# H3 and squared-ReLU layers in fp32 on one core: operands, residuals and rows of a joint unit of 1024 tokens are moved in time and place

## The chip, the cores and the metric

The kernel runs on one core of one Trainium2 chip. The metric is the device time of one execution in microseconds (us); lower is better. PE is TensorE, DVE VectorE, ACT ScalarE, POOL GpSimd, and SP the queue engine that issues the transfers.

## The reference

Two equal layers over 2048 tokens of width 1024. Each is an H3 block and a squared-ReLU MLP, with residuals:

```python
def H3(q, k, v):            # q = layernorm(x); A_k, A_v, A_shift_k, A_ssm_k, A_ssm_D are inputs
    kv = causal_conv4(k, shift_k) * v
    y = long_causal_conv(kv, ssm_k) + kv * ssm_D        # per channel, over 2048 tokens
    return q * y
def MLP(x):                 # w1 is 1024 x 3584, w2 is 3584 x 1024
    r = relu(x @ w1 + b1)
    return (r * r) @ w2 + b2
for _ in range(2):
    x = x + H3(layernorm(x), ...)
    x = x + MLP(layernorm(x))
```

All is fp32. The change touches the MLP only.

## The kernel before

**Matmuls.** An fp32 operand is held as two fp32r tiles: hi, a rounded copy that ACT writes, and lo, the raw value minus hi, a subtraction on DVE or POOL. A product is three matmuls, hi·hi, hi·lo and lo·hi (`mm3`, L344 to L346); each of the three moves 512 columns. The program is a list of steps, one for each weight tile of 128x512, and a step is 12 matmuls.

**Units.** The MLP runs in units of (layer, 512 tokens), in an order written out by hand. Units 5 and 6, the last block of layer 0 and the third of layer 1, are one joint unit of 1024 tokens, multiplied in the manner of Strassen and Winograd with seven products instead of eight. It has three parts:

- *Part 1* (`ja`, a = 1 and 2, 28 steps): for each of 14 pairs p of hidden blocks, x11·w11 and then x12·w21 in the same bank. After the first, ACT copies the bank (`j_p1`, L1906) and the copy goes to memory (PD, L1907); after the second, ACT rectifies the sum (L1901, L1902) and `j_c11` stores it as a result (RD, L1912). Meanwhile the other block's rows are loaded (`j_rows_load`), normalised on ACT (`j_rows_norm`, L1853) and turned (L1873), and DVE makes sums of blocks for part 2.
- *Part 2* (`ja`, a = 6, 5, 7, 4, 3, 70 steps): five more products for each p, with weights that are sums of four blocks of w1. The blocks are loaded at L1057, two into the ring `wr` and two into `jr`, with one more row of the ring for the fifth sum; DVE makes the sums (L1045 to L1048). ACT copies product 6's bank (`j_keep`, L1924) before product 7 goes on in it. Seven combined results go to memory as operands of part 3.
- *Part 3* (`jb`): seven products, in the order 0, 4, 5, 2, 1, 6, 3, of 14 steps each. `r_advance` loads their operands (L1970), ACT casts hi (L1981), and DVE or POOL subtracts (L1989), into a ring of 4 tiles for product 0 and of 7 later; from product 1's middle on (n ≥ 70) every second subtraction is POOL's. After each product `j_evict` (L2037, DVE) adds its banks into one of four residual groups: product 0 into (0,0), 4 into (1,1), 5 and 2 into (0,1), 1 into (0,0) again, 6 into (1,1), 3 into (1,0). The residuals come by `j_acc_load` (L2016) into `acc`, `yh`, `yl`, `fy` and `fg`, b2 by `load_b2` (L1825) into `px`; POOL adds b2 (`j_b2`, L2024). Products 0, 5, 6 and 3 use one side of four banks, 4, 2 and 1 the other, so a side's next product waits for the eviction of its last one. After product 1, `j_next` puts the next unit's norms and combination (L705 to L723, L819, L820) on DVE.

**What sets the order.** `lag.at(n, f)` runs f n steps later; within a step the program issues due work, weights, then operands. Weights are loaded eight steps ahead, cast four ahead (L1101) and subtracted three ahead (L1109). A weight used more than once is kept in memory as a split pair after its first use (WD): such a pair is loaded whole, 512 KB (L1097), unless it is in the set `single`; a raw tile is 256 KB. Raw tiles, blocks for sums and the results of `j_c11` share the ring `wr` of eight rows (`row()`). All these transfers go through SP's one queue in program order, and each engine works through its own list in order.

Of the kernel before, what the change touches and what calls it, by code (L numbers as in the profile page):

```python
# [11 lines left out]
F32 = mybir.dt.float32  # L12
F32R = mybir.dt.float32r
# [6 lines left out]
S, D, F = 2048, 1024, 3584  # L20
P = 128
T = 512
NT = T // P
NB = S // T
KT = D // P
FT = F // P
FC = 7
# [8 lines left out]
ORDER = [(0, 0), (1, 0), (0, 1), (0, 2), (1, 1), (0, 3), (1, 2), (1, 3)]  # L36
# [17 lines left out]
JU = 5  # L54
WMAKE = 4
NP = FT // 2
# [4 lines left out]
R_LOAD, R_HI, R_LO = 8, 4, 3  # L61
# [187 lines left out]
def tile_h3_mlp(ctx: ExitStack, tc: tile.TileContext, q, kT, vT, shk, ssmT, ssmD, w1, b1, w2, b2,  # L249
                fwd_t, pro_t, inv_t, sgn_t, out):  # L250
    nc = tc.nc
    V, A, G, PE, SY = nc.vector, nc.scalar, nc.gpsimd, nc.tensor, nc.sync
# [4 lines left out]
    cv = ctx.enter_context(tc.tile_pool(name="cv", bufs=1))  # L257
# [9 lines left out]
    X1 = [dram.tile([P, NT, D], F32, name=f"x1{b}") for b in range(NB)]  # L267
# [12 lines left out]
    def mkfg(shape, dt=F32):  # L280
        return cv.tile(shape, dt, name="fg", bufs=3)
# [246 lines left out]
    def prod_stream():  # L528
# [381 lines left out]
    steps, wsrc, single = [], [], set()  # L910

    def add(kind, u, c, a, i, tts=ALL, w=None):
        if w is None:
            w = len(wsrc)
            wsrc.append((kind, c, a, i))
        steps.append((kind, u, c, a, i, tts, w))
# [17 lines left out]
    def add_joint(u):  # L934
        for n in range(0, NP, 2):
            for kh in range(2):
                for p in (n, n + 1):
                    wsrc.append(("m1", 2 * p // FC, 2 * p % FC, kh))
                    add("ja", u, 0, kh + 1, p, w=len(wsrc) - 1)
        seq = [(6, 0), (5, 0), (7, 0)]  # L940
        for p in range(NP):
            more = p + 1 < NP
            seq += [(6, p + 1)] * more + [(4, p), (3, p)] + [(5, p + 1), (7, p + 1)] * more
        for j, p in seq:
            wsrc.append(("s", 0, j, p))
            add("ja", u, 0, j, p, w=len(wsrc) - 1)
        for j in JORD:
            for p in range(NP):
                f = 2 * p + (j > 0)
                wsrc.append(("m2", f // FC, int(j == 2), f % FC) if j < 3 else ("t", p, (j - 4) % 4, 0))  # L950
                add("jb", u, 0, j, p, w=len(wsrc) - 1)
# [194 lines left out]
    mw = ctx.enter_context(tc.tile_pool(name="mw", bufs=1))  # L1146
# [689 lines left out]
    rowp, xop, jst, jrows, jacc, rt, rptr = [], {}, {}, [], {}, {}, {"load": 0, "hi": 0, "lo": 0}  # L1836

    def jrow():
        if not rowp:
            n = jst["n"] = jst.get("n", -1) + 1  # L1840
            t = pre.tile([P, D], F32, name="px", bufs=2) if n % 3 == 2 else ml.tile([P, D], F32, name="acc", bufs=NT)
            rowp.extend((t[:, 0:512], t[:, 512:]))
        return rowp.pop(0)

    def j_rows_load(b):
        for tt in range(NT):
            jrows.append(ml.tile([P, D], F32, name="acc", bufs=NT))
            SY.dma_start(jrows[tt], X1[b][:, tt])

    def j_rows_norm(rn, tt):  # L1850
        for h in range(2):
# [55 lines left out]
        SY.dma_start(PD[p], t)  # L1907

    def j_c11(o, p):
        x = row()  # L1910
        rectify(x["t"], o, 2 * p)
        SY.dma_start(RD[0][p], x["t"])  # L1912
        drop(x)
# [42 lines left out]

    rseq = [(j, p) for j in JORD for p in range(NP)]

    def r_ring(n):
        return 4 if n < NP else 7  # L1960

    def r_load():
        n = rptr["load"]
        rptr["load"] += 1
        if n == 0:
            jst["xr"] = mw.tile([P, 8, T], F32, name="xh", bufs=1)
            jst["xs"] = mw.tile([P, 4, 2, T], F32R, name="xl", bufs=1)
        t = jst["xr"][:, n % 8] if n < NP else ml.tile([P, T], F32, name="rh", bufs=FC + 1)
        j, p = rseq[n]
        SY.dma_start(t, RD[j][p])  # L1970
        rt[n] = [t]

    def r_hi():
        n = rptr["hi"]
        rptr["hi"] += 1
        if n < NP:
            t = jst["xs"][:, n % 4]
        else:
            nm, m = (("cx", 2), ("cg", 2), ("cp", 3), ("cx", 2), ("cp", 3), ("cg", 2), ("cp", 3))[n % 7]
            t = cv.tile([P, 2, T], F32R, name=nm, bufs=m)  # L1980
        A.copy(t[:, 0], rt[n][0])  # L1981
        rt[n].append(t)

    def r_lo():
        n = rptr["lo"]
        rptr["lo"] += 1
        raw, t = rt[n]
        E = G if n >= 5 * NP and n % 2 else V
        E.tensor_sub(t[:, 1], raw, t[:, 0].bitcast(F32))  # L1989

    def r_advance(m):
        N = len(rseq)
        while rptr["lo"] < rptr["hi"] and rptr["lo"] <= m + R_LO:
            r_lo()
        while rptr["hi"] < min(rptr["load"], N) and rptr["hi"] <= m + R_HI and rptr["hi"] - r_ring(rptr["hi"]) < m:
            r_hi()
        while rptr["load"] < N and rptr["load"] <= m + R_LOAD and rptr["load"] - 8 < rptr["lo"]:
            r_load()
        while m >= 0 and rptr["lo"] <= m:
            if rptr["load"] <= rptr["hi"]:  # L2000
                r_load()
            if rptr["hi"] <= rptr["lo"]:
                r_hi()
            r_lo()
        rt.pop(m - 1, None)

    def j_acc_load(k):
        if k == 0:
            ts = [ml.tile([P, D], F32, name="acc", bufs=NT) for _ in range(NT)]
        else:  # L2010
            ts = [cv.tile([P, D], F32, name=nm, bufs=1) for nm in ("yh", "yl", "fy")]
        for tt in range(NT):
            for h in range(2):
                d = slice(h * 512, (h + 1) * 512)
                a = jacc[k, tt, h] = ts[tt][:, d] if tt < len(ts) else mkfg([P, T])
                SY.dma_start(a, X1[ORDER[JU + k][1]][:, tt, d])  # L2016
        if k == 0:
            jst["acc"] = ts

    def j_b2(st, k):  # L2020
        for tt in range(NT):
            for h in range(2):
                a = jacc[k, tt, h]
                G.tensor_add(a, a, st["t"][:, h * 512:(h + 1) * 512])  # L2024

    def j_banks(j):
        if j in JOPEN or j in (5, 6, 3, 2):
# [90 lines left out]
    for sb in range(1, NB):  # L2118
        if WIN[sb] > lo_u:
# [3 lines left out]
            n = sum(last_step[u] + 1 - start_step[u] - 19 * (1 - PREP_PACE) for u in range(lo_u, hi_u))  # L2123
# [16 lines left out]
    for s, (k, u, c, a, i, tts, w) in enumerate(steps):  # L2140
        if s < 2 * AHEAD_0:
            continue
        l, b = ORDER[u]
        if u != cur_u:
            cur_u = u
            if u:
                xT = nxt[0] if u == JU + 2 else nxt
            bst = {}
            if u == JU:
                jb = ORDER[JU + 1][1]  # L2150
                lag.at(5, j_rows_load, jb)
                lag.at(10, j_places)
                for tt in range(NT):
                    lag.at(8 + tt // 2, j_rows_norm, rn, tt)
                    lag.at(11 + 3 * tt, j_flip, tt)
                    lag.at(12 + 3 * tt, j_xsums, tt, xT, 0)
                    lag.at(13 + 3 * tt, j_xsums, tt, xT, 1)
            elif u in WINO:
                wacc, rp = {}, {}
                lag.at(11, load_wacc, wacc, b)  # L2160
                lag.at(34, load_b2, bst)
                lag.at(38, add_b2w, bst, wacc)
            else:
                if not (u and direct[u - 1]):
                    accs = []
                    lag.at(5, load_acc, accs, b)
                lag.at(12, load_b2, bst)
                lag.at(16, add_b2, bst, accs)
# [17 lines left out]
        if k == "m1":  # L2186
# [3 lines left out]
            xh, xl = xT  # L2190
# [5 lines left out]
            for kk in range(4):  # L2196
                t = slice(kk * P, (kk + 1) * P)
# [8 lines left out]
        elif k == "ja":  # L2206
            if a < 3:
# [3 lines left out]
                xs, ys = ([x[:, 4 * (a - 1) + kk] for kk in range(4)] for x in xT)  # L2211
            else:
                o = jst[i]["b" if a in (6, 7, 4) else "e"]
                xs, ys = xop[a]
            opens = a in (1, 5)
            for kk in range(4):
                t = slice(kk * P, (kk + 1) * P)
# [15 lines left out]
                    lag.at(d, j_out, i, nm)  # L2233
        elif k == "jb":
            if s == jb_at:
                lag.at(8, j_acc_load, 0)
                lag.at(7, j_acc_load, 1)
                lag.at(9, load_b2, bst)
                lag.at(13, j_b2, bst, 0)
                lag.at(14, j_b2, bst, 1)  # L2240
            if i == 0:
                os = j_banks(a)
            hi, lo = (rt[s - jb_at][1][:, n] for n in range(2))
            for tt in range(NT):
                t = slice(tt * P, (tt + 1) * P)
# [7 lines left out]
        elif k == "w2":  # L2253
# [6 lines left out]
            hi, lo = rp[i][a]  # L2260
            for n in range(2):
                t = slice(n * P, (n + 1) * P)
# [11 lines left out]
        else:  # L2274
# [5 lines left out]
            for tt in tts:  # L2280
                t = slice(tt * P, (tt + 1) * P)
# [66 lines left out]
        while todo > 0:  # L2348
            x = next(pds, 0)
# [62 lines left out]
```

## Time and profile before

| what | value |
|---|---|
| time, median of three runs | 2698.43 us (2697.25 to 2702.56) |
| profiled execution | 2697.74 us, its span 2695.9 us |
| mean granted clock of TensorE | 0.992 |
| busy, share of the span: PE, DVE, ACT, POOL | 97%, 73%, 41%, 32% |
| moved over the span | 283 GB/s |

In the rows of windows, each engine has its busy time and, in brackets, its instructions; PEclk is the granted clock. In the waits, a row gives who waited for whom: us in total, how often, and the longest. In the timeline a row is an instruction's start, duration, engine, line, name, tiles and shapes, and in brackets the idle time before it and what ended it.

Part 1 is at 1826.8 to 1911.8 us, part 2 up to 2112.6, and part 3's products begin at 2112.6, 2150.7, 2200.5, 2238.6, 2276.6, 2314.7 and 2360.4.

### The profile page before, as it was taken

What the parts mean: (1) busy time and instruction counts of PE and PEld (TensorE: products, weight loads), DVE (VectorE), ACT (ScalarE), POOL (GpSimd) and SP (SyncE); (2) the same over time, 40 slices, a digit from 0 to 9 for tenths busy, and PEclk for the clock granted to TensorE, in tenths of its full rate; (3) what the DMA queues carried; (4) which work ended last, traced back from release to release, by engine and by line L of the source; (5) the groups of instructions that cost most, each with busy time, mean ns of one, the idle gap of its engine ahead of it and who ended that gap; (6) DMA issues with size and microseconds to landing.
All of it is one profiled execution on the core that took longest, in us unless ns stands there. A gap on an engine that the chain in (4) does not pass through costs nothing.

```text
span 2695.9 us, 36188 instructions
## 1 busy us (share of the span) xinstructions
PE 2625.7 (97%) x12400; PEld 2199.5 (82%) x12400; DVE 1972.1 (73%) x2968; ACT 1112.2 (41%) x1936; POOL 869.8 (32%) x546
## 2 busy tenths in 40 slices
PE   8999999999999999999999999999999989999999
PEld 7888787888888888888888888887788878788887
DVE  7878888788987887779677678565688464745565
ACT  4454344433444233442234422255565343345443
POOL 2336565355632655337553364000000030111000
PEclk9999999999999999999999999999999999999999
DMA  8789898699989898788987878689889977756556
GB/s 258 260 303 319 291 313 279 229 308 378 328 307 322 303 340 295 257 333 291 351 273 264 313 290 328 237 277 324 278 295 312 379 230 273 273 177 201 177 169 206
DMA packets 390680, 764.47 MB, mean 284 GB/s; under 512 B 45392, under 2 KB 160736, under 8 KB 390496
## 3 DMA queue, kind: packets, MB, share of 16 engines
q1 hardware_dynamic: 390496, 762.16, 82.3%
q8 instruction: 98, 1.61, 0.2%
q14 instruction: 86, 0.70, 0.1%
HBM read 584.80 MB, written 177.21 MB: 283 GB/s over the span
## 4 chain that ended last, share of the span: by engine, by line
PE 74%; DVE 10%; DMA 9%; issue 2%; SPq 2%; ACT 1%; POOL 1%; DVEq 0%; ACTq 0%; POOLq 0%
PE p L344 22%; PE p L345 22%; PE p L346 22%; DMA wr<-w 3%; PE p L1187 2%; DVE whl L1109 2%; DMA whl<-wd_m 1%; PE pt L344 1%; PE pt L345 1%; PE pt L346 1%; DMA wd_m<-whl 1%; DVE sm L538 1%; DMA cg<-gd 1%; DVE st L705 0%; PE pt L400 0%
## 5 line engine op out<-in xcount | busy, mean ns | idle before, releaser
L534 POOL TENSOR_TENSOR cp<-cx,cg 128x384 f32<-128x384 f32 (+5 forms) x288 | 545.8, 1908 | 571.6 <-DVE sm L538 383.5
L344 PE MATMUL p<-xh,whl 128*128 128x512 f32 (+1 forms) x1504 | 576.6, 383 | 3.8 <-DMA whl<-wd_m 3.7
L346 PE MATMUL p<-xh,whl 128*128 128x512 f32 (+1 forms) x1504 | 572.4, 381 | 0.8 <-POOL whl L1109 0.8
L345 PE MATMUL p<-xl,whl 128*128 128x512 f32 (+1 forms) x1504 | 572.4, 381 | 0.1
L1109 DVE TENSOR_TENSOR whl<-wr,whl 128x512 fp32r<-128x512 f32 x524 | 444.6, 861 | 120.0 <-ACT whl L1101 118.4
L1101 ACT CAST whl<-wr 128x512 fp32r<-128x512 f32 x539 | 328.9, 620 | 437.7 <-PE p L346 271.1
L344 PE MATMUL p<-whl,rh 128*128 128x512 f32 x1204 | 475.3, 395 | 5.5 <-ACT whl L1101 4.4
L345 PE MATMUL p<-whl,rh 128*128 128x512 f32 x1204 | 470.7, 391 | 1.7 <-DVE whl L1109 1.1
L346 PE MATMUL p<-whl,rl 128*128 128x512 f32 x1204 | 470.4, 391 | 0.0
L344 PEld LDWEIGHTS p<-xh,whl 128*128 128x128 f32 x1504 | 283.5, 188 | 57.2 <-DMA whl<-wd_m 4.5
L346 PEld LDWEIGHTS p<-xh,whl 128*128 128x128 f32 x1504 | 283.1, 188 | 55.5 <-POOL whl L1109 1.0
L345 PEld LDWEIGHTS p<-xl,whl 128*128 128x128 f32 x1504 | 283.5, 188 | 52.2 <-DVE xl L1500 0.3
L344 PEld LDWEIGHTS p<-whl,rh 128*128 128x128 f32 x1204 | 227.2, 189 | 52.5 <-ACT whl L1101 5.3
L345 PEld LDWEIGHTS p<-whl,rh 128*128 128x128 f32 x1204 | 227.1, 189 | 48.4 <-DVE whl L1109 2.3
L346 PEld LDWEIGHTS p<-whl,rl 128*128 128x128 f32 x1204 | 226.9, 188 | 47.7
L1594 DVE TENSOR_TENSOR rl<-wr,rh 128x512 fp32r<-128x512 f32 x140 | 141.8, 1014 | 164.7 <-ACT rh L1589 164.3
L538 DVE TENSOR_REDUCE sm<-cp 128x128 f32<-128x384 f32 (+5 forms) x288 | 249.8, 874 | 11.7 <-POOL cp L534 11.7
L1586 ACT ACTIVATE wr<-p,b1t 128x512 f32<-128x512 f32 x138 | 95.3, 690 | 357.1 <-PE p L346 354.4
L2024 POOL TENSOR_TENSOR acc<-acc,px 128x512 f32<-128x512 f32 x8 | 9.9, 1281 | 464.5 <-DMA wr<-td 464.5
L1709 DVE TENSOR_TENSOR acc<-p,acc 128x512 f32<-128x512 f32 x152 | 100.0, 686 | 75.2 <-PE p L346 75.2
L684 POOL TENSOR_TENSOR sm<-sm 128x512 f32<-128x512 f32 x48 | 69.2, 1441 | 129.6 <-DVE sm L538 116.7
L1587 ACT ACTIVATE wr<-wr 128x512 f32<-128x512 f32 x140 | 88.8, 634 | 4.4
(413 smaller groups left out, 4172.4 us busy)
## 6 DMA issues: line engine op xcount, KB each, us to landing
whl<-wd_m SPq DMA_DIRECT2D x345, 512.0 KB, 5.4
wr<-w SPq DMA_DIRECT2D x429, 256.0 KB, 5.4
wd_m<-whl SPq DMA_DIRECT2D x70, 512.0 KB, 5.9
wr<-td SPq DMA_DIRECT2D x104, 256.0 KB, 4.4
cx<-xd SPq DMA_DIRECT2D x48, 512.0 KB, 6.0
cg<-gd SPq DMA_DIRECT2D x48, 512.0 KB, 6.8
rh<-rd SPq DMA_DIRECT2D x84, 256.0 KB, 5.5
gd<-fg SPq DMA_DIRECT2D x72, 256.0 KB, 5.8
```

Source lines behind the costliest of these rows:

```text
L344: PE.matmul(o, lh, rh, start=start, stop=False, skip_group_check=skip)
L345: PE.matmul(o, lh, rl, start=False, stop=False, skip_group_check=skip)
L346: PE.matmul(o, ll, rh, start=False, stop=stop, skip_group_check=skip)
L534: G.tensor_mul(pr.rearrange("p c i -> p i c"), xt[:, 0:j + 1], gt[:, j::-1])
L538: V.tensor_reduce(sm[:, ty, jj], st["pr"], axis=AX.X, op=OP.add)
L684: E.tensor_add(s[:, 1:3], s[:, 1:3], s[:, 0:1].to_broadcast([P, 2, s.shape[2]]))
L1101: A.copy(t[:, 0], raws[n]["t"])
L1109: ENG[e[n % len(e)]].tensor_sub(t[:, 1], raws[n]["t"], t[:, 0].bitcast(F32))
L1586: A.activation(r, st["o"], AF.Relu, bias=b1t[:, st["f"]:st["f"] + 1])
L1587: A.activation(r, r, AF.Square)
L1594: V.tensor_sub(st["lo"], st["r"]["t"], st["hi"].bitcast(F32))
L1709: V.tensor_add(accs[tt][:, d], o, accs[tt][:, d])
```

## The change

Five edits, all in the joint unit:

1. **Weights of part 1.** For the first eight pairs p, both weights join `single`: they come raw and are split again. Eleven of these 16 came as kept pairs before.
2. **Rows.** `j_rows_load` takes one row of 512 KB at a time, 4 to 7 steps in (all four were at step 5), and `j_rows_norm` one row a step, 7 to 10 steps in (8, 8, 9, 9 before).
3. **Other places.** The results of `j_c11` for the last four pairs (p from 10 to 13) lie in places from `jrow()` and no longer in the ring `wr`.
4. **Operands of part 3.** The look-ahead of the casts grows from 4 steps to 14, between the third product's end and the fifth's middle (m = 42 to 62), and loads and subtractions follow it. A list of up to 15 free tiles takes the place of the two rings; from m = 84 on the seven tiles in `cv` are given back. All subtractions are DVE's.
5. **Residuals and b2.** A residual group is loaded as four pieces of 256 KB, one a step: (0,0) at 8 to 11 steps, (1,1) at 13 to 16, (0,1) at 18 to 21, (1,0) at 23 to 26. b2 is loaded at 8. POOL adds it to (0,0) at 18 to 21, to (1,1) at 23 to 26, to (0,1) at 28 to 31, to (1,0) at 33 to 36. For (0,0) that is behind product 0's eviction, which was behind the b2 sum before.

```diff
                 for p in (n, n + 1):
                     wsrc.append(("m1", 2 * p // FC, 2 * p % FC, kh))
+                    if p < 8:
+                        single.add(len(wsrc) - 1)
                     add("ja", u, 0, kh + 1, p, w=len(wsrc) - 1)
...
     def j_c11(o, p):
-        x = row()
+        x = row() if p < 10 else {"t": jrow()}
...
-    def r_ring(n):
-        return 4 if n < NP else 7
+    def r_look(m):
+        return R_HI + min(max(m - 42, 0) // 2, 10)
...
+        free = jst["free"]
+        x = min(free, key=lambda x: x[0] if n >= 5 * NP else -x[0])
+        free.remove(x)
+        A.copy(x[1][:, 0], rt[n][0])
+        rt[n] += [x[1], x]
...
-        E = G if n >= 5 * NP and n % 2 else V
-        E.tensor_sub(t[:, 1], raw, t[:, 0].bitcast(F32))
+        V.tensor_sub(t[:, 1], raw, t[:, 0].bitcast(F32))
...
-                lag.at(5, j_rows_load, jb)
                 lag.at(10, j_places)
                 for tt in range(NT):
-                    lag.at(8 + tt // 2, j_rows_norm, rn, tt)
+                    lag.at(4 + tt, j_rows_load, jb, tt)
+                    lag.at(7 + tt, j_rows_norm, rn, tt)
...
-                lag.at(8, j_acc_load, 0)
-                lag.at(7, j_acc_load, 1)
-                lag.at(9, load_b2, bst)
-                lag.at(13, j_b2, bst, 0)
-                lag.at(14, j_b2, bst, 1)
+                lag.at(8, load_b2, bst)
+                for n, (x, h) in enumerate(((0, 0), (1, 1), (0, 1), (1, 0))):
+                    lag.at(7 + 5 * n, j_acc_load, x, h)
+                    for tt in range(NT):
+                        lag.at(18 + 5 * n + tt, j_b2, bst, x, tt, h)
```

On SP's queue at the seam of parts 1 and 2, where `pd` is the store of a first product's copy, `rd_10` and `rd_11` stores of `j_c11`, and `wr` and `jr` the four blocks of a weight sum, before:

```order
L1907 DMA pd_254<-fx 128x512
L1057 DMA wr<-w 128x512 x2
L1057 DMA jr<-w 128x512 x2
L1916 DMA fg<-pd_243 128x512
L1912 DMA rd_10_155<-wr 128x512
L1631 DMA td_135<-sm 128x2x256 x2
L1912 DMA rd_11_156<-wr 128x512
L1907 DMA pd_255<-fx 128x512
L1612 DMA sm<-w 128x2x256 x2
L1916 DMA fg<-pd_244 128x512
L1907 DMA pd_256<-fx 128x512
L1057 DMA wr<-w 128x512 x2
```

The same place now:

```order
L1908 DMA pd_254<-fx 128x512
L1059 DMA wr<-w 128x512 x2
L1059 DMA jr<-w 128x512 x2
L1917 DMA fg<-pd_243 128x512
L1913 DMA rd_10_155<-acc 128x512
L1633 DMA td_135<-sm 128x2x256 x2
L1913 DMA rd_11_156<-acc 128x512
L1908 DMA pd_255<-fx 128x512
L1059 DMA wr<-w 128x512 x2
L1059 DMA jr<-w 128x512 x2
L1614 DMA sm<-w 128x2x256 x2
L1917 DMA fg<-pd_244 128x512
```

The second group of blocks moved from behind the store of `pd_256` to right behind that of `pd_255`, and the two results come out of `acc`.

On SP's queue in part 3's product 0, where `x_108` and `x_109` are the residuals, `rh` an operand and `wr<-td` a weight, before:

```order
L1086 DMA wr<-td_131 128x512
L1970 DMA rh<-rd_0_201 128x512
L1631 DMA td_144<-sm 128x2x256 x2
L2016 DMA yh<-x_108 128x512 x2
L2016 DMA yl<-x_108 128x512 x2
L2016 DMA fy<-x_108 128x512 x2
L2016 DMA fg<-x_108 128x512 x2
L1086 DMA wr<-td_132 128x512
L1970 DMA rh<-rd_1_202 128x512
L2016 DMA acc<-x_109 128x512 x8
L1086 DMA wr<-td_133 128x512
L1970 DMA rh<-rd_2_203 128x512
```

The same place now:

```order
L1088 DMA wr<-td_131 128x512
L1980 DMA rh<-rd_0_201 128x512
L1633 DMA td_144<-sm 128x2x256 x2
L1088 DMA wr<-td_132 128x512
L1980 DMA rh<-rd_1_202 128x512
L1827 DMA px<-b 128x1024
L2032 DMA acc<-x_109 128x512
L1088 DMA wr<-td_133 128x512
L1980 DMA rh<-rd_2_203 128x512
L2032 DMA acc<-x_109 128x512
L1088 DMA wr<-td_134 128x512
L1980 DMA rh<-rd_3_204 128x512
```

Sixteen residual pieces in two bursts became one piece between a step's weight and operand, and b2 (`px`) moved ahead of them all.

On POOL from product 0's b2 sums on, where `px` is b2, `acc` to `fg` are residuals, and `cg` and `cx` are operand tiles, before:

```order
L2024 TENSOR_TENSOR acc<-acc,px 128x512 x8
L2024 TENSOR_TENSOR yh<-yh,px 128x512 x2
L2024 TENSOR_TENSOR yl<-yl,px 128x512 x2
L2024 TENSOR_TENSOR fy<-fy,px 128x512 x2
L2024 TENSOR_TENSOR fg<-fg,px 128x512 x2
L1989 TENSOR_TENSOR cg<-rh,cg 128x512
L1989 TENSOR_TENSOR cx<-rh,cx 128x512
```

The second half of the b2 sums on the same engine now, and what follows it:

```order
L2036 TENSOR_TENSOR acc<-acc,px 128x512 x4
L2036 TENSOR_TENSOR yh<-yh,px 128x512
L2036 TENSOR_TENSOR yl<-yl,px 128x512
L2036 TENSOR_TENSOR fy<-fy,px 128x512
L2036 TENSOR_TENSOR fg<-fg,px 128x512
L1688 TENSOR_TENSOR acc<-acc,px 128x512 x6
```

The sums come in groups of four pieces, and the 14 operand subtractions that stood behind them are gone from POOL: the next unit's b2 sum follows at once.

More of the change, by code (lines that the diff above doesn't have):

```diff
@@ L1843, in jrow, with j_rows_load @@
         return rowp.pop(0)
[L1845 to L1848, printed above, removed]
+    def j_rows_load(b, tt):
+        jrows.append(ml.tile([P, D], F32, name="acc", bufs=NT))
+        SY.dma_start(jrows[tt], X1[b][:, tt])
     def j_rows_norm(rn, tt):
@@ L1965, in r_load @@
         if n == 0:
-            jst["xr"] = mw.tile([P, 8, T], F32, name="xh", bufs=1)
-            jst["xs"] = mw.tile([P, 4, 2, T], F32R, name="xl", bufs=1)
-        t = jst["xr"][:, n % 8] if n < NP else ml.tile([P, T], F32, name="rh", bufs=FC + 1)
+            x = mw.tile([P, KT, T], F32, name="xh", bufs=1)
+            jst["raw"] = [x[:, i] for i in range(8)]
+            x = mw.tile([P, 4, 2, T], F32R, name="xl", bufs=1)
+            jst["free"] = jst["x"] = [(1, x[:, i]) for i in range(4)]
+        elif n == NP:
+            jst["raw"] = [ml.tile([P, T], F32, name="rh", bufs=FC + 1) for _ in range(8)]
+            for nm, m in (("cx", 2), ("cg", 2), ("cp", 3)):
+                jst["free"] += [(0, cv.tile([P, 2, T], F32R, name=nm, bufs=m)) for _ in range(m)]
+        elif n == 2 * NP:
+            x = mw.tile([P, 4, 2, T], F32R, name="xh", bufs=1)
+            jst["free"] += [(1, x[:, i]) for i in range(4)]
+        t = jst["raw"][n % 8]
         j, p = rseq[n]
@@ L1975, in r_hi, with r_room @@
         rptr["hi"] += 1
[L1976 to L1982, printed above, removed]
+        free = jst["free"]
[3 more added lines that the diff above has]
+        rt[n] += [x[1], x]
+    def r_room():
+        n = rptr["hi"]
+        return any(n < 6 * NP or not x[0] for x in jst["free"])
     def r_lo():
@@ L1986, in r_lo @@
         rptr["lo"] += 1
-        raw, t = rt[n]
-        E = G if n >= 5 * NP and n % 2 else V
-        E.tensor_sub(t[:, 1], raw, t[:, 0].bitcast(F32))
+        raw, t = rt[n][:2]
+        V.tensor_sub(t[:, 1], raw, t[:, 0].bitcast(F32))
     def r_advance(m):
         N = len(rseq)
-        while rptr["lo"] < rptr["hi"] and rptr["lo"] <= m + R_LO:
+        if m - 1 in rt:
+            jst["free"].append(rt.pop(m - 1)[2])
+        while rptr["lo"] < rptr["hi"] and rptr["lo"] <= m + r_look(m) - 1:
             r_lo()
-        while rptr["hi"] < min(rptr["load"], N) and rptr["hi"] <= m + R_HI and rptr["hi"] - r_ring(rptr["hi"]) < m:
+        while rptr["hi"] < min(rptr["load"], N) and rptr["hi"] <= m + r_look(m) and r_room():
             r_hi()
-        while rptr["load"] < N and rptr["load"] <= m + R_LOAD and rptr["load"] - 8 < rptr["lo"]:
+        while rptr["load"] < N and rptr["load"] <= m + r_look(m) + 4 and rptr["load"] - 8 < rptr["lo"]:
             r_load()
@@ L2004, in r_advance, with j_acc_load, j_acc_part, j_b2 @@
             r_lo()
[L2005 to L2011, printed above, removed]
-        for tt in range(NT):
[L2013 to L2024, printed above, removed]
+    def j_acc_load(k, h):
+        if "acc" not in jst:
+            jst["acc"] = [ml.tile([P, D], F32, name="acc", bufs=NT) for _ in range(NT)]
+        elif "bcc" not in jst:
+            jst["bcc"] = [cv.tile([P, D], F32, name=nm, bufs=1) for nm in ("yh", "yl", "fy")]
+            jst["bcc"].append([mkfg([P, T]) for _ in range(2)])
+        for tt in range(NT):
+            lag.at(1 + tt, j_acc_part, k, tt, h)
+    def j_acc_part(k, tt, h):
+        d = slice(h * 512, (h + 1) * 512)
+        t = jst["acc"][tt] if k == 0 else jst["bcc"][tt]
+        a = jacc[k, tt, h] = t[h] if isinstance(t, list) else t[:, d]
+        SY.dma_start(a, X1[ORDER[JU + k][1]][:, tt, d])
+    def j_b2(st, k, tt, h):
+        a = jacc[k, tt, h]
+        G.tensor_add(a, a, st["t"][:, h * 512:(h + 1) * 512])
     def j_banks(j):
```

## The prediction

> **What bounds the kernel now.** I read the busy shares first (TensorE 97% of the span), then the windows of the joint unit by stage, then TensorE's waits there, and last the timeline at each wait. The windows:
>
> ```profile
> core 0: us, PE busy (x) PEld busy (x) DVE busy (x) ACT busy (x) POOL busy (x), PEclk, DMA share, GB/s
> 1826.80:1911.80 85.00, 81.89 (x370) 67.29 (x368) 49.17 (x87) 49.75 (x85) 0.00 (x0) 0.98 0.93 328
> ...
> 2112.60:2150.70 38.10, 38.10 (x169) 31.54 (x168) 17.15 (x28) 12.49 (x21) 0.00 (x0) 1.00 1.05 397
> 2150.70:2200.50 49.80, 40.84 (x170) 32.69 (x169) 32.06 (x37) 19.86 (x34) 23.43 (x16) 0.90 0.84 285
> 2200.50:2238.60 38.10, 38.10 (x170) 31.56 (x169) 18.69 (x30) 13.95 (x24) 0.00 (x0) 1.00 0.64 209
> ...
> 2314.70:2360.40 45.70, 38.26 (x169) 31.38 (x168) 44.52 (x89) 19.50 (x36) 9.48 (x7) 0.96 0.68 222
> ```
>
> Product 0 (the row at 2112.60) is 14 steps of 12 matmuls in 38.10 us: 0.2268 us a matmul, 2.72 us a step, no gap. That is the floor. Product 4 took 49.80 us, 11.7 more, and product 6 45.70, 7.6 more, each for the same 168 matmuls. So the joint unit is bound by TensorE's own rate with a few holes, and only closing or opening holes changes the time. The holes by cause:
>
> ```profile
> PE p L345 <- DVE whl L1109: 7.9, 1, 7.9
> PE p L344 <- DVE yh L2037: 7.4, 1, 7.4
> PE p L344 <- ACT fx L1924: 4.7, 2, 4.0
> PE p L344 <- DMA whl<-wd_m: 3.0, 1, 3.0
> PE p L344 <- DVE acc L1930: 1.3, 2, 0.9
> ```
>
> A hole costs more than its wait:
>
> ```profile
> 1848.36 0.39 PE L346 MATMUL p<-xh,whl 128*128 128x512 f32 x1
> 1851.75 0.80 PE L344 MATMUL p<-xh,whl 128*128 128x512 f32 x1 [3.00 <-DMA whl<-wd_m]
> 1852.34 0.63 PE L345 MATMUL p<-xl,whl 128*128 128x512 f32 x1
> 1852.77 0.63 PE L346 MATMUL p<-xh,whl 128*128 128x512 f32 x1
> ...
> 1854.88 0.39 PE L345 MATMUL p<-xl,whl 128*128 128x512 f32 x1
> ...
> 1917.01 0.39 PE L346 MATMUL p<-fy,whl 128*128 128x512 f32 x1
> 1921.41 0.79 PE L344 MATMUL p<-rl,whl 128*128 128x512 f32 x1 [4.01 <-ACT fx L1924]
> ...
> 1926.62 0.39 PE L344 MATMUL p<-rh,whl 128*128 128x512 f32 x1
> ```
>
> After the 3.0 us wait starts are 0.43 apart, not 0.23, until 1854.88. From 1848.36 to 1854.88 are 6.52 us for eight matmuls that need 1.81: hole A costs **4.7**. From 1917.01 to 1926.62 are 9.61 us for 13 that need 2.95: hole B costs **6.7**. Hole C is the windows' **11.7**. Hole D is 7.6 and, after it, a slow tail:
>
> ```profile
> 2352.58 0.39 PE L346 MATMUL pt<-whl,cp 128*128 128x512 f32 x1
> 2360.41 0.77 PE L344 MATMUL p<-whl,cx 128*128 128x512 f32 x1 [7.44 <-DVE yh L2037]
> ...
> 2363.49 0.39 PE L345 MATMUL pt<-whl,cx 128*128 128x512 f32 x1
> ```
>
> Seven matmuls in 3.08 us instead of 1.59: 1.5 more, **9.1** in all. A to D make 32.2 us. Some smaller holes of part 2 (the waits' 1.3 at L1930 among them) come to about 4 more; no edit reaches those.
>
> **The change part by part.**
>
> *Edits 1 and 2, hole A.* TensorE waits for a kept pair from memory. What else moved there:
>
> ```profile
> acc<-x SPq DMA_DIRECT2D x4, 512.0 KB, 7.4
> whl<-wd_m SPq DMA_DIRECT2D x4, 512.0 KB, 8.0
> ...
> 1845.20 3.08 ACT L1853 ACTIVATE acc<-acc,rn 128x512 f32<-128x512 f32 x4 [1.27 <-DMA acc<-x]
> ```
>
> Four rows of 512 KB are issued in one step with four pairs, and a pair takes 8.0 us to land. A pair is loaded at the cast's place in the program, four steps ahead (10.9 us), behind the rows. Afterwards the weight is raw, half the bytes, loaded eight steps ahead (21.8 us), and rows come one a step. The wait goes; I leave 0.5 (0 to 3). The price is 11 more casts and subtractions. Part 1 has 35 us of 85 free on ACT and 36 on DVE (first window); 11 × 0.62 = 6.8 us of casts and 11 × 0.69 = 7.6 of subtractions, by these rows:
>
> ```profile
> 1918.49 0.62 ACT L1101 CAST whl<-wr 128x512 fp32r<-128x512 f32 x1 [7.86 <-DVE wr L1047]
> ...
> 1916.31 0.69 DVE L1045 TENSOR_TENSOR wr<-wr 128x512 f32<-128x512 f32 x1 [7.38 <-DMA wr<-w]
> ```
>
> So they cost nothing while the weights stay ahead; without that cover they are the slower rival below. The norms were four in a step, 3.08 us of ACT (L1853), in two steps; now two, 1.5 us, in each of four steps, ahead of part 1's bank copies. With casts and rectifying, ACT may then be busy for over 2.72 us in a step or two: I add 0.5 (0 to 4).
>
> *Edit 3, hole B.* The two rows above tell it. The second group of blocks landed late, DVE idled 7.38 us for it, ACT stood 7.86 us at the cast of the sum, and the bank copy behind that cast on ACT (L1924) was what TensorE waited for. The blocks were late because their ring rows were held by results:
>
> ```profile
> 1906.18 0.33 SPq L1907 DMA_DIRECT2D pd<-fx  x1
> 1906.61 2.90 SPq L1612 DMA_DIRECT2D sm<-w  x2
> ...
> 1910.66 0.94 SPq L1057 DMA_DIRECT2D wr<-w  x2
> ```
>
> Now those loads stand right behind the first of these rows, at 1906.6 instead of 1910.66: 4.05 us earlier, against a hole of 4.2 (1917.01 to 1921.41, less one matmul). What is late next is the same copy, by little; I leave 0.7 (0 to 4, if the four block loads, now ahead of two others, land no sooner).
>
> *Edit 5, hole C.* Product 0's eviction waits on DVE for POOL's b2 sums, and weights' subtractions queue behind it:
>
> ```profile
> 2156.71 9.89 POOL L2024 TENSOR_TENSOR acc<-acc,px 128x512 f32<-128x512 f32 x8 [464.52 <-DMA wr<-td]
> ...
> 2165.41 0.69 DVE L2037 TENSOR_TENSOR acc<-pt,acc 128x512 f32<-128x512 f32 x1 [1.76 <-POOL acc L2024]
> 2166.02 1.13 DVE L1109 TENSOR_TENSOR whl<-wr,whl 128x512 fp32r<-128x512 f32 x1
> 2167.07 1.75 DVE L1989 TENSOR_TENSOR cx<-rh,cx 128x512 fp32r<-128x512 f32 x1
> ```
>
> The eviction was due at 2150.7, but POOL began at 2156.71, since b2 came last on the queue, behind sixteen pieces. Now no b2 sum stands before this eviction. Its residuals are issued one a step from step 8 to 11, three steps (8 us) ahead at least. I leave 0.5 (0 to 5). The new wait: group (1,1) has its sums at steps 23 to 26 and product 4's eviction at 28; 1.7 us of POOL each, in 2.72 us of step, end ahead of it. Beside POOL a DVE operation with two inputs takes 1.75 us instead of 0.69, 1.06 more; 16 sums could so cost DVE 17 us over products 4 and 5, where it is idle for 18 (49.80 − 32.06) and 19 (38.10 − 18.69): nothing to TensorE.
>
> *Edit 4, hole D.* In product 6's window DVE is busy for 44.52 of 45.70 us: the eviction is late because DVE is full with the next unit's norms, not because it waits. Between the two evictions DVE does, before and after, 14 weight and 7 operand subtractions; those POOL did are made earlier, in products that leave DVE half idle. What goes is only POOL's company:
>
> ```profile
> 2332.26 0.75 DVE L819 SCALAR_TENSOR_TENSOR px<-acc,mv,px 128x512 f32<-128x512 f32 x1
> 2333.04 1.67 DVE L820 SCALAR_TENSOR_TENSOR acc<-px,rs,acc 128x512 f32<-128x512 f32 x1
> ...
> 2338.19 1.28 POOL L1989 TENSOR_TENSOR cp<-rh,cp 128x512 fp32r<-128x512 f32 x1 [4.03 <-DVE cg L1989]
> ...
> L721 DVE SCALAR_TENSOR_TENSOR rt<-rs,ve x24: 219/220/2115, 803.2 to 2365.6; 128x1 f32<-128x1 f32 x24
> 2338.26 1.22 DVE L721 SCALAR_TENSOR_TENSOR rt<-rs,ve 128x1 f32<-128x1 f32 x1
> ...
> 2359.57 0.69 DVE L2037 TENSOR_TENSOR yh<-p,yh 128x512 f32<-128x512 f32 x1
> ```
>
> Each of six POOL subtractions stretches one DVE operation by 0.5 to 1.08 us (1.22 against a median of 0.22; 1.67 against 0.75), 5.5 in sum. The eviction then starts at 2354.1 and frees the bank by 2354.9; TensorE would go on at 2352.81. A wait of 2.1 stays, with perhaps a slow tail: I leave 2.6 (0 to 9). The Trainium skill, "SBUF — State Buffer", section "Who interferes with whom", says that a VectorE instruction with two SBUF inputs contends with a GpSimd one that reads SBUF, and that the loser fully blocks. The trace agrees in kind; by full blocking for 1.3 us a time I estimate 7.8 us and no hole D at all (the third rival), while the rows' 5.5 leave one. The same rule speaks against spreading the b2 sums, priced above.
>
> Sum: A 4.7 → 0.5, B 6.7 → 0.7, C 11.7 → 0.5, D 9.1 → 2.6, and 0.5 new: 32.2 − 4.3 = 27.9 less, 0.5 more, **27.4**. The profiled execution took 2697.74 us (its span 2695.9), so 2670.3; the median of the runs is 0.7 above it: **2671**.
>
> **The rivals.**
>
> - *Hole D stays whole.* DVE is as full as before, and an eviction that slips back by other DVE work of the same step gives 6.5 back: 2678. Against: the stretched rows.
> - *A new wait in part 1 or under products 0 to 5*, a norm ahead of a bank copy, a residual that lands late: the size of one of A or B twice over, 9 to 10 us: 2681. For: DMA is busy for 0.93 of part 1 and 1.05 in product 0.
> - *All holes go.* By full blocking the 2.6 of D go, with the leftovers of A to C and the new wait (2.2): 2666, or 2663 with most of part 2's small holes.
> - *The change doesn't do it:* the holes move to the next late thing: 2693 to 2703.
> - *Slower.* The 11 newly split weights become the bound: raw rows wait for free places in the ring of eight, so a load is issued two steps (5.4 us) ahead instead of eight and takes the 8.0 us of the row above. Each then costs 2.6 and a slow tail of 1.5 as at A, 4.1; eleven make 45: 2716. It decides from 27.4 / 11 = 2.5 us each. Against: ACT and DVE idle four tenths of part 1, the raw weights there caused none of the five waits, and half the bytes go.
>
> A word on the tails: the Trainium skill, "TensorE: Matmul & The Clock Gate", Part 1, says that an idle window of about 3.4 us, free-running, halves the clock. By it a 2.1 us wait at D may stay without a tail; the trace shows tails behind 3.0 and 4.0.
>
> **How the numbers follow.** Forecast (2666 to 2677) 0.53; D whole 0.12; a new wait 0.13; all holes gone 0.10; no change 0.04; slower 0.08. A measurement of this kernel can tell about 0.2%, 5.4 us, from no change. So faster 0.88, same 0.04, slower 0.08. The range 2662 to 2685 takes in the first four cases with the ends of A's and C's leftovers.
>
> **What would show it.** Right: product 4's window near 38.1 and no row L2037 waiting for POOL; no wait for `wd_m`, L1924's below 1 us; product 6 near 40 us, no POOL operation in it and L721 at 0.22. Wrong: TensorE waiting for ACT or DVE (L1101, L1109) in part 1, a wait for `acc` from memory at product 0's end, or product 6's window still above 44.

## The result, and the profile after

| | before | changed |
|---|---|---|
| median of four runs each | 2699.82 us (2697.25 to 2702.56) | 2678.97 us (2678.68 to 2679.88) |
| profiled execution, span | 2697.74, 2695.9 us | 2678.93, 2677.1 us |
| ratio | | 0.9923, interval 0.9906 to 0.994 |

The change is faster by 0.77%, 20.9 us between the medians and 18.8 between the profiled executions. The forecast was 2671, so 27.4 us: the way held, and the size was a third too large. The measured time lies inside the whole range, 2662 to 2685, and 2 us outside the forecast's own part of it, 2666 to 2677.

The windows of the changed kernel's joint unit, cut at the same matmuls as before: part 1, part 2, then products 0, 4, 5, 2, 1, 6, 3:

```profile
core 0: us, PE busy (x) PEld busy (x) DVE busy (x) ACT busy (x) POOL busy (x), PEclk, DMA share, GB/s
1828.30:1913.30 85.00, 81.42 (x369) 66.09 (x368) 54.68 (x96) 53.17 (x93) 0.00 (x0) 1.00 0.83 292
1913.30:2108.30 195.00, 192.72 (x841) 156.94 (x841) 154.95 (x265) 113.47 (x195) 0.00 (x0) 1.00 0.92 310
2108.30:2146.40 38.10, 38.10 (x169) 31.55 (x169) 19.93 (x32) 15.46 (x26) 0.99 (x1) 1.00 1.04 392
2146.40:2184.50 38.10, 38.10 (x169) 31.53 (x168) 33.80 (x33) 15.49 (x27) 22.96 (x16) 1.00 1.04 382
...
2298.70:2340.80 42.10, 38.30 (x170) 31.40 (x169) 39.31 (x89) 15.83 (x29) 0.00 (x0) 0.98 0.66 205
2340.80:2385.00 44.20, 44.20 (x201) 36.65 (x202) 23.74 (x44) 17.58 (x31) 0.00 (x0) 0.94 0.35 117
```

Part 1 takes 85.00 us as before. Part 2 is 5.8 us shorter (200.80 before). Product 4 stands at the floor, 11.7 shorter. Product 6 is 3.6 shorter and product 3 1.0 longer. That makes 20.1 us for the unit; 1.3 of them are lost in the stretches before and behind it. Part 1 begins 1.5 us later than before, and that start is noise of this size: it lies at 1828.3 and at 1830.4 us in two traces of the changed kernel, and from 1826.0 to 1832.1 in all traces here. TensorE's waits in the unit now:

```profile
PE p L344 <- DVE yh L2049: 3.8, 1, 3.8
PE p L344 <- ACT fx L1907: 2.9, 3, 1.5
PE p L344 <- DVE px L1931: 1.2, 3, 0.7
PE p L344 <- ACT fx L1925: 1.1, 2, 0.7
PE pt L1874 <- ACT acc L1854: 0.5, 1, 0.5
```

The waits of 7.9 (C) and 3.0 (A) are gone, B's (L1925 now) is 0.7 us at the longest, D's (L2049) is halved, and two are new: for part 1's bank copies (L1907), and for a norm ahead of the turning (L1854). At hole B the block loads are issued 79.8 us after the start of part 1, where it was 83.8 before: 4.1 us earlier, as forecast. At hole C no eviction of DVE (L2049) waits for POOL any more, only one of them for a late residual. The first row is from SP's queue, the second from DVE's waits between 2100 and 2190 us:

```profile
1908.12 0.93 SPq L1059 DMA_DIRECT2D wr<-w  x2
...
DVE acc L2049 <- DMA acc<-x: 0.8, 1, 0.8
```

### The profile page after: what moved, and what is told of

It is laid out like the page before. It is cut to its first block, busy times and chain, and to the rows that moved or that the text cites. A ratio compares the mean times of both kernels' runs of the same rounds, so it can differ in the third digit from the quotient of the medians.

```text
span 2677.1 us, 36183 instructions
## 1 busy us (share of the span) xinstructions
PE 2621.7 (98%) x12400; PEld 2195.7 (82%) x12400; DVE 1987.5 (74%) x2993; ACT 1116.0 (42%) x1947; POOL 851.7 (32%) x532
## 3 DMA queue, kind: packets, MB, share of 16 engines
q8 instruction: 98, 1.61, 0.2%
## 4 chain that ended last, share of the span: by engine, by line
PE 76%; DVE 9%; DMA 8%; issue 2%; SPq 2%; ACT 2%; POOL 1%; DVEq 0%; ACTq 0%; POOLq 0%
PE p L344 22%; PE p L345 22%; PE p L346 22%; DMA wr<-w 3%; PE p L1189 2%; PE pt L345 2%; PE pt L344 2%; PE pt L346 2%; DVE whl L1111 1%; DMA whl<-wd_m 1%; DMA cx<-xd 1%; DMA cg<-gd 0%; DVE st L705 0%; SPq L1955 0%; PE pt L429 0%
## 5 line engine op out<-in xcount | busy, mean ns | idle before, releaser
L1111 DVE TENSOR_TENSOR whl<-wr,whl 128x512 fp32r<-128x512 f32 x535 | 452.2, 858 | 95.6 <-ACT whl L1103 82.6
L1103 ACT CAST whl<-wr 128x512 fp32r<-128x512 f32 x550 | 334.7, 618 | 383.0 <-PE p L346 243.8
L2036 POOL TENSOR_TENSOR acc<-acc,px 128x512 f32<-128x512 f32 x8 | 11.7, 1481 | 454.0 <-DMA wr<-td 451.0
L1688 POOL TENSOR_TENSOR acc<-acc,px 128x512 f32<-128x512 f32 x6 | 7.7, 1318 | 267.6 <-DMA px<-b 267.6
```

The lines of the kernel that those rows point to most:

```text
L1103: A.copy(t[:, 0], raws[n]["t"])
L1111: ENG[e[n % len(e)]].tensor_sub(t[:, 1], raws[n]["t"], t[:, 0].bitcast(F32))
```

## The experiments

**Each edit alone.** Four kernels are the one before with one edit, or with 1 and 2 together. They ran beside one another and beside 27 runs of the kernel before (median 2701.27).

`only_residuals` is edit 5: `j_acc_load`, `j_acc_part`, `j_b2` and the lines of the schedule at the end of the diff above.

> The kernel before with edit 5 alone (residuals in pieces, b2 ahead, b2 sums late). My theory: each hole belongs to one edit and closes without the others, so product 4's window falls from 49.8 to about 38.2 us and the time by 11 to 12 us, to about 2687; holes A, B and D stay at 4.7, 6.7 and 9.1. Rival: hole C closes only because edit 4 also brings operands earlier (the wait that followed the weight's was for an operand's subtraction, L1989); then 1.5 to 3 us of the 11.7 stay and the gain is 9 to 10.

2686.16 us, ratio 0.9955 (0.9942 to 0.9969). In its trace, the stretch from product 0's start to product 4's end is 11.7 us shorter, as in the changed kernel. Its waits:

```profile
PE p L344 <- DVE yh L2037: 7.4, 1, 7.4
PE p L344 <- ACT fx L1924: 5.1, 2, 4.4
PE p L344 <- DMA whl<-wd_m: 2.6, 1, 2.6
```

D, B and A stand as before, and C is missing whole: the rival, that edit 4 had a share in it, falls. Which of edit 5's three steps does it (the pieces, b2 ahead of them, or the sum behind the eviction) is not separated.

`only_places` is edit 3:

```diff
-        x = row()
+        x = row() if p < 10 else {"t": jrow()}
```

> The kernel before with edit 3 alone (four results of part 1 in other places than the ring). My theory: hole B at the seam of parts 1 and 2 (6.7 us) falls to about 0.7 and the time by 5 to 6 us, while hole A (the wait for a kept pair) stays at 4.7. Rival: the blocks of the second weight sum came early in the changed kernel because the ring was fuller of raw weights or the rows' transfers were spread; then hole B stays above 4 us here and the time falls by less than 3.

2693.18 us, ratio 0.9973 (0.9965 to 0.9982), so 7 us, a little above the 5 to 6 expected. The wait at L1924 is 1.3 us in two, 0.7 the longest:

```profile
PE p L344 <- DMA whl<-wd_m: 2.6, 1, 2.6
PE p L344 <- ACT fx L1924: 1.3, 2, 0.7
```

The places alone close B; neither the raw weights nor the spread rows are needed for it.

`only_part1` is edits 1 and 2.

> The kernel before with edits 1 and 2 alone (raw weights for the first eight pairs, rows and norms one a step). My theory: hole A (4.7 us) goes, and in its place come waits for bank copies at L1906 and for a norm of the order that the changed kernel shows (0.5, 1.4, 1.7, 0.7 us), about 4 us together, so the time stays within 2 us of before; hole B stays 6.7 or grows by up to 1. Rival: the new waits of part 1 come from edit 3's use of other tiles; then they are missing here, and the time falls by 4 to 5.

2701.19 us, ratio 1.0009 (0.9999 to 1.0018): no gain. The wait for a kept pair is gone, and in its place stand these:

```profile
PE p L344 <- ACT fx L1907: 3.2, 3, 1.5
...
PE pt L1874 <- ACT acc L1854: 1.2, 1, 1.2
```

They are the changed kernel's own new waits, so they come from edits 1 and 2 and not from edit 3's tiles. Hole B stayed (3.6 at L1925).

`only_operands` is edit 4 (`r_look`, the free list, all subtractions on DVE).

> The kernel before with edit 4 alone (operands up to 14 steps ahead, all subtractions on DVE). My theory: the wait at product 6's eviction falls from 7.6 to about 4 us, as DVE loses 5.5 us of stretching by POOL and gains one idle stretch of 1.6 us behind a cast on ACT that waits for TensorE to give a tile free; the slow tail behind it stays 1.5 to 2.5; holes A, B and C stay, so the time falls by 2.5 to 4 us. Rival: the idle 1.6 us in the changed kernel came from elsewhere (transfers of the residuals or of the rows); then it is missing here and the wait is near 2.2.

2694.85 us, ratio 0.9987 (0.9977 to 0.9997), 3.5 us. The wait at product 6's eviction is 3.8 us, and DVE's idle 1.6 us before it is there too, so neither the residuals nor the rows cause it. By the ratios the four gains are 12.1, 7.3, −2.4 and 3.5 us, 20.5 together against 20.9 for the whole. That they add is not shown by it: each interval reaches 2 to 4 us to either side, and by the medians the gains are 15.1, 8.1, 0.1 and 6.4, 29.7 together. What the traces show is that each edit acts on its own hole and leaves the other three standing.

**Part 1: which of edits 1 and 2 makes the new waits.** `pairs_back` is the changed kernel without edit 1:

```diff
-                    if p < 8:
-                        single.add(len(wsrc) - 1)
```

> The changed kernel with edit 1 undone (the eleven weights come as kept pairs again; rows and norms stay one a step). Theory 1: the new waits for bank copies (1.7, 0.7 and 0.9 us) come from the eleven splits, which keep DVE from the block sums that ACT waits for (L1888); they go, and hole A returns only in part, up to 1.5 us, since the rows no longer burst; the time falls by 2 to 3 us to about 2676. Theory 2: the new waits come from the norms' new places; they stay at 3 to 4 us, hole A comes back with 2 to 5 us, and the time is 2680 to 2684.

2675.69 us, ratio 0.991 (0.9896 to 0.9923): theory 1, with its number. The interval overlaps the changed kernel's, so the trace has to decide. Its wait in part 1, then the window of its part 1, from that part's first matmul to part 2's:

```profile
PE p L344 <- DMA whl<-wd_m: 1.2, 1, 1.2
...
1829.00:1911.10 82.10, 80.80 (x369) 66.22 (x368) 49.16 (x88) 49.63 (x85) 0.00 (x0) 1.00 0.94 344
```

Part 1 takes 82.1 us instead of 85.0. One trace has one execution, but the others agree: in the seven traces with eight raw pairs (the changed kernel's two and that of `rows_back` below among them) part 1 takes 85.0 to 86.3 us, and in the three with two raw pairs or none, and the rows spread, 82.1 to 82.8. No wait for the bank copies is left, and of hole A 1.2 us return without slow steps behind them (2.6 to 2.8 with edit 3, 4 or 5 alone). So spreading the rows shrank hole A, and the raw weights, which took the rest, cost more than that. How they cost it is seen on ACT where the block sums are made, first in the changed kernel, then in `pairs_back`:

```profile
ACT rh L1889 <- DVE px L1888: 5.1, 2, 2.7
```

```profile
ACT rh L1887 <- DVE px L1886: 3.6, 3, 1.6
```

ACT stands at the cast of a block sum that DVE hasn't made, 2.7 us the longest instead of 1.6, while DVE is busy for 23.38 of the 24 us from 1866 to 1890 (22.04 in `pairs_back`). Part 1's bank copy is behind that cast on ACT:

```profile
1872.40 0.62 ACT L1889 CAST rh<-px 128x512 fp32r<-128x512 f32 x1 [2.41 <-DVE px L1888]
1872.93 0.58 ACT L1892 COPY px<-pt 128x512 f32<-128x512 f32 x1
1873.40 0.59 ACT L1907 COPY fx<-p 128x512 f32<-128x512 f32 x1
...
1874.04 0.50 PE L344 MATMUL p<-xh,whl 128*128 128x512 f32 x1 [1.49 <-ACT fx L1907]
```

Two of the three waits, 1.5 and 0.5 us, come this way. The third, 0.9 us at the end of part 1, has another cause: there DVE itself idles for 3.1 us until blocks of a weight sum land.

`rows_back` is the changed kernel without edit 2 (rows in one step, norms at 8, 8, 9, 9).

> The changed kernel with edit 2 undone (four rows in one step, norms two rows a step at 8 and 9; the weights stay raw). Theory 1 (splits make the new waits): the waits at L1907 stay at 3 us, only the wait of the turning for a norm (0.5, with its slow steps 1.4) goes, and the raw weights come in time without the spread rows: time within 1.5 us of the changed kernel. Theory 2 (norms' places make them): the waits at L1907 fall below 1 us and the time by 2 to 3. Third: raw weights land late behind the burst of rows, a wait of 2 us or more at L1103 in part 1, and the time rises by 3 to 5.

2679.13 us, ratio 0.9925 (0.9913 to 0.9938), the changed kernel's time. The waits for the bank copies (L1908 here) stay, 4.1 us in five instead of 2.9 in three, and the norm's goes, as theory 1 has it; no raw weight is late:

```profile
PE p L344 <- ACT fx L1908: 4.1, 5, 1.4
```

**Hole D: what is left of it.** On DVE in the changed kernel, from product 1's eviction (2296.91) to product 6's (2339.96) are 43.05 us, with one idle stretch, and on ACT at the same time:

```profile
2312.79 1.29 DVE L1111 TENSOR_TENSOR whl<-wr,whl 128x512 fp32r<-128x512 f32 x2
2315.70 0.69 DVE L2000 TENSOR_TENSOR cp<-rh,cp 128x512 fp32r<-128x512 f32 x1 [1.61 <-ACT cp L1989]
...
2339.96 0.68 DVE L2049 TENSOR_TENSOR yh<-p,yh 128x512 f32<-128x512 f32 x1
```

```profile
2315.04 0.62 ACT L1989 CAST cp<-rh 128x512 fp32r<-128x512 f32 x1 [1.83 <-PE pt L345]
```

Before, it was 46.69 us without a gap (2312.88 to 2359.57). The cast waits for a tile that TensorE is still reading. Which tiles it may take is written in the changed kernel:

```python
    def r_room():
        n = rptr["hi"]
        return any(n < 6 * NP or not x[0] for x in jst["free"])
```

`x[0]` is 0 for the seven tiles in `cv` and 1 for the eight others. The operands from n = 84 on, product 3's, are cast during product 6 and may only go into those seven, each as TensorE's last step leaves it. So it is the eight others that are given back, where edit 4 above names the seven.

`ahead12` changes the look-ahead's end from 14 steps to 12:

```diff
-        return R_HI + min(max(m - 42, 0) // 2, 10)
+        return R_HI + min(max(m - 42, 0) // 2, 8)
```

> The changed kernel with the operands up to 12 steps ahead instead of 14, so that two of the fifteen tiles are free when a cast is due. My theory: at 14 each cast takes the tile that TensorE has just left, so ACT waits for TensorE and DVE for ACT, 1.6 us once while the norms are due; with 12 that idle goes, DVE runs without a gap from product 1's eviction to product 6's, the wait there falls from 3.8 to about 2.2 us, and the time by 1.5 to 4 us (more if the slow tail of 2.4 goes with it). Rival: the idle is not due to the tile; the wait stays 3.5 to 4 and the time the same.

2680.83 us, ratio 0.9927 (0.9914 to 0.9941): no gain. DVE's idle stretch is gone, as expected, but not for the reason expected. The casts still wait for TensorE, since the tiles that are free are not in `cv`:

```profile
2314.37 0.62 ACT L1989 CAST cp<-rh 128x512 fp32r<-128x512 f32 x1 [1.32 <-PE pt L345]
```

This cast comes 15.4 us behind product 1's eviction instead of 18.1, when DVE still has other work to do. The wait at product 6's eviction is 3.5 us. DVE's operand subtractions between the two evictions, here and in the changed kernel:

```profile
2298.90:2341.70 42.80, 6.17 (x9) 0.99 0.75 228
```

```profile
2296.90:2339.90 43.00, 4.80 (x7) 0.99 0.70 215
```

A shorter look-ahead leaves two more subtractions for the full window, 1.4 us, which eat the 1.6 us of idle time. So two more ready operands are worth as much to DVE as the idle stretch cost it.

`drain` does not refill the stock in that window:

```diff
-        return R_HI + min(max(m - 42, 0) // 2, 10)
+        x = R_HI + min(max(m - 42, 0) // 2, 10)
+        return max(R_HI, min(x, 6 * NP - m)) if 5 * NP <= m < 6 * NP else x
```

> The changed kernel with the look-ahead not refilled during product 6 (steps 70 to 83): it shrinks to four steps, so that three operand subtractions fewer stand between the two evictions on DVE (three more after them) and most casts wait for no tile. My theory: 3 times 0.6 us and the 1.6 us of idle time go from the 43.0 us between the evictions; the wait falls from 3.8 to about 0.4 us without a slow tail, and the time by 4 to 6 us, to about 2674. Rival: DVE fills up with other due work at once (the norms come as early as DVE lets them), and the wait stays over 2 us.

The wait is 2.6 us, without a slow tail: the rival's size, but not by its mechanism. Four subtractions are left instead of seven, but DVE doesn't fill up with other work. It idles for 2.0 us at a weight's subtraction whose cast on ACT waits for TensorE, with the combination behind it in its list, so not all of the work saved comes off the end:

```profile
2310.68 0.69 DVE L1111 TENSOR_TENSOR whl<-wr,whl 128x512 fp32r<-128x512 f32 x1
2313.40 0.69 DVE L1111 TENSOR_TENSOR whl<-wr,whl 128x512 fp32r<-128x512 f32 x1 [2.03 <-ACT whl L1103]
```

Its five runs lie from 2674.86 to 2683.22 (median 2679.88, ratio 0.9923, 0.991 to 0.9935): too wide to tell 4 us from none. Here the trace decides and not the time.

**A better version.** The next three ran with the changed kernel once more on one chip.

> The changed kernel once more, on the same chip as the next two. Within 2 us of 2679 and 20 to 22 us under the kernel before; the wait at product 6's eviction is 3.8 us again, its slow tail between 1.4 and 3 us.

2679.73 us, ratio 0.9925 (0.9913 to 0.9938), the wait 3.8 again. `drain_early` is `drain` with the combination a step earlier:

```diff
-            for k, d in enumerate((8, 9, 10)):
+            for k, d in enumerate((7, 8, 9)):
```

> The kernel with the shrinking look-ahead, and the combination of the next unit one step earlier (7, 8 and 9 steps after product 1 instead of 8, 9 and 10). My theory: DVE's work between the two evictions is 39.8 us there, and the other 2.0 us are idle because the combination is put in at its step and not before; one step earlier fills them, and the wait at product 6's eviction falls from 2.6 to 0.6 us, without a tail; 4 to 6 us under the changed kernel run beside it. Rival: the combination waits for other things (its loads, the norms on ACT), the idle only moves, and the wait stays above 2.

2678.5 us, ratio 0.9919 (0.9905 to 0.9932): not 4 to 6 us. DVE's idle time went, but the last quarter's norm, two operations of L705, moved ahead of the eviction with it. On ACT the square root of that norm (L713) waits for DVE, and the weight that TensorE waits for is cast behind it, so 2.1 us stay:

```profile
2342.28 0.29 ACT L713 ACTIVATE sd<-mv,epst 128x1 f32<-128x1 f32 x1 [4.01 <-DVE mv L706]
2342.48 0.60 ACT L1103 CAST whl<-wr 128x512 fp32r<-128x512 f32 x1
...
PE p L344 <- ACT whl L1103: 2.1, 1, 2.1
```

The eviction's first operation on DVE ends at 2342.97, a tenth of a microsecond before that cast, so both would have to move.

`two_pairs` is `drain_early` with raw weights only where a kept pair had been late:

```diff
-                    if p < 8:
+                    if p in (4, 5):
```

> The same, with raw weights for the pairs p = 4 and 5 alone instead of the first eight: the wait for a kept pair was met at p = 4 in the kernel before and at p = 5 with the pairs back. My theory: with few splits DVE has the block sums in time, so the waits at L1907 (3 us) go, and no wait for a kept pair comes: 2 to 4 us under drain_early, 7 to 9 under the changed kernel, about 2671. Rival: another kept pair of the first eight is late now, by 1 us or more, and the gain is under 2 us.

2673.54 us, ratio 0.9902 (0.9887 to 0.9917): 5 us under `drain_early`, 6 under the changed kernel, and all of its four runs lie below all of theirs. Part 1 takes 82.8 us instead of `drain_early`'s 85.8. L1907's waits fall to 0.7 us, and no wait for a kept pair is left. `last_behind` adds this:

```diff
-            for k, d in enumerate((7, 8, 9)):
+            for k, d in enumerate((7, 8, 9) if tt < 3 else (9, 10, 11)):
```

> two_pairs with the last quarter's combination, norm and scale two steps later (9, 10 and 11 steps plus its place, the first three quarters at 7, 8, 9), so that they stand behind product 6's eviction. My theory: of the 41.3 us between the evictions on DVE 4.5 us move behind the second (four operations of 0.75 at L819 and L820, 1.3 of L705), DVE has time to spare, and the square root on ACT (L713), behind which a weight's cast stood, moves too; the wait of 2.1 us at product 6's end goes, with its slow tail of 1.6, and nothing is late in product 3, where DVE is idle for 19 us: 2 to 4 us under two_pairs, about 2670. Rival: the last quarter is then late for the turning at the next unit's start, and TensorE waits there (L2085 of before) by 2 us or more.

2672.08 us, ratio 0.9892 (0.9875 to 0.9908). Product 6 stands at the floor, and now the eviction waits for TensorE:

```profile
2299.60:2337.70 38.10, 38.10 (x170) 31.53 (x169) 35.71 (x83) 14.99 (x28) 0.00 (x0) 1.00 0.66 210
...
2337.67 0.69 DVE L2050 TENSOR_TENSOR yh<-p,yh 128x512 f32<-128x512 f32 x1 [1.22 <-PE p L346]
```

Hole D is closed, and the next unit's start isn't late for it: TensorE has no wait from 2290 to 2470 us. The time can't be told from `two_pairs` (the intervals overlap); both beat the changed kernel, by 6 to 8 us between the medians.

## Why the prediction was right, and where its size was off

| term | forecast: hole before to after | measured |
|---|---|---|
| A, with the new waits of part 1 | 4.7 to 1.0 | part 1's window 85.00 before and after: 0 gained |
| B | 6.7 to 0.7 | part 2 5.8 shorter |
| C | 11.7 to 0.5 | 11.7 to 0 |
| D | 9.1 to 2.6 | products 6 and 3 together 2.6 shorter: about 6.5 left |
| outside the unit | 0 | 1.3 longer in the profiled execution |

So A gave 3.7 us less than forecast and D 3.9 less. The number still came out inside the range because the range took in two rivals, D whole (2678) and a new wait (2681), and about half of each came true. That the measured 2679 stands beside both of their numbers is chance.

- *B and C* went by the mechanism named. `only_places` and `only_residuals` each closed one hole alone and left the rest.
- *A was mis-sized in its price, not in its gain.* The step that failed is "they cost nothing while the weights stay ahead". The weights did stay ahead, with no wait at L1103 or L1111 in part 1; the slower rival's raw weights landing late did not come. But the free 35 us on ACT and 36 on DVE are a mean over a stage. Where the block sums are made, DVE had next to none to spare even before (busy for 22.63 of the 24 us from 1865 to 1889): there a split delays a sum, the sum ACT's cast, and the cast a bank copy. I had put the new wait down to the norms, at 0.5 us; the splits made most of it (`pairs_back`), the norms the smaller part (`rows_back`). This is the "new wait in part 1" rival, at 4 to 5 us instead of 9 to 10: it took back all of A.
- *D was mis-sized by 3.9 us.* What POOL's company cost was right: 46.69 − (43.05 − 1.61) = 5.25 us against 5.5. The failed step is "What goes is only POOL's company", with nothing new late. In product 6's window each cast takes a tile in `cv` that TensorE has just left; that tied DVE to TensorE for 1.61 us in a window where it has no slack. Most of the rest is the slow tail: the forecast's 2.6 left 0.5 for it beside a wait of 2.1, and it took 2.4:

```profile
2336.60 0.39 PE L346 MATMUL pt<-whl,xl 128*128 128x512 f32 x1
2340.79 0.77 PE L344 MATMUL p<-whl,cx 128*128 128x512 f32 x1 [3.80 <-DVE yh L2049]
2341.35 0.63 PE L345 MATMUL p<-whl,cx 128*128 128x512 f32 x1
...
2345.93 0.39 PE L344 MATMUL p<-whl,cx 128*128 128x512 f32 x1
```

- *The rule on the shared port* (the Trainium skill, "SBUF — State Buffer", "Who interferes with whom") agrees in kind. In amount the measurement decides: 5.25 us came off DVE with POOL's subtractions, not the 7.8 of full blocking, and the third rival fell with it. The spread b2 sums agree in kind too: all sixteen had run by the end of product 4, where 33 instructions kept DVE busy for 33.80 of 38.10 us, while 30 took 18.61 in product 5 without POOL. TensorE never waited, as forecast, but with 4.3 us of slack left on DVE. The forecast had counted 18 there, in a window that hole C itself made 11.7 us longer, and had counted on product 5 as well; so "nothing to TensorE" came true with less room than it claimed.

## What to carry to other kernels

Slack is to be read at the step where the work lands and on the queue where it stands, not as a stage's mean: eleven splits, each a cast of 0.6 us and a subtraction of 0.7, cost some 3 us in a stage in which both their engines were idle four tenths of the time. Where an engine is full, count its instructions between the two events that matter and then ask what each of them waits for; a longer look-ahead turns into a wait for a place, so count the places that the next operand is allowed to use, and not all that are free. A remedy that costs work belongs only where the wait was seen: raw weights for eight pairs gave back what they gained, and with the rows spread part 1 was as short with raw weights for two pairs (82.8 us) or for none (82.1).

## What the runs showed of the hardware that was not expected

The slow stretch after a wait doesn't follow the wait's length. Behind 7.4 us seven matmuls were slow (before). Behind the same 3.8 us they were twelve in the changed kernel, fourteen in `pairs_back` and seven in `only_operands`. In `two_pairs` a wait of 2.06 us was followed first by four matmuls near full speed and then by eight at 0.43 us, at a granted clock of 0.50 (2336.34 to 2339.73):

```profile
2335.34 0.47 PE L344 MATMUL p<-whl,cx 128*128 128x512 f32 x1 [2.06 <-ACT whl L1103]
2335.64 0.40 PE L345 MATMUL p<-whl,cx 128*128 128x512 f32 x1
...
2336.75 0.63 PE L346 MATMUL p<-whl,cx 128*128 128x512 f32 x1
...
2339.99 0.39 PE L345 MATMUL p<-whl,cx 128*128 128x512 f32 x1
```

In `drain_early` the same wait of 2.1 us cost no slow step. The Trainium skill, "TensorE: Matmul & The Clock Gate", Part 1, has the clock halved after an idle window of about 3.4 us, and the window free-running, so that the place of a wait in it counts as well as its length. The seven, twelve and fourteen behind one length agree with that. That a wait of 2.06 us, shorter than the window, cost a slow stretch, and one that began 1.0 us after the work went on, does not follow from it; there the measurement decides.
